# Attention block on one core: a quarter of x transposed by TensorE and the rest by transfers, output weights loaded late, order of work picked among 24

## The chip, the core and the metric

The kernel runs on one core of a Trainium2 chip. The metric is device time in microseconds (us), as the median of repeated executions. One further execution was taken with the hardware profiler; views of the profile are from it. Engines are named as in the profile: PE is TensorE (matmuls), PEld its weight loads, DVE is VectorE, ACT is ScalarE, POOL is GpSimd, SP is SyncE, which here only issues transfers (DMAs). "L298" is line 298 of the kernel.

## The reference

Multi-head self-attention in bfloat16, with S = 2048 positions, D = 448 channels, 16 heads of 28 channels:

```python
B, S, D, H = 1, 2048, 448, 16
Dh = D // H
qkv = (x @ wqkv).reshape(B, S, 3, H, Dh).transpose(2, 0, 3, 1, 4)
q, k, v = qkv[0], qkv[1], qkv[2]
scores = jnp.einsum("bhqd,bhkd->bhqk", q, k) * (Dh ** -0.5)
p = _softmax(scores, axis=-1)
o = jnp.einsum("bhqk,bhkd->bhqd", p, v)
return o.transpose(0, 2, 1, 3).reshape(B, S, D) @ wo
```

## The kernel before

**Tiling.** The 16 heads form four groups g of four (G, HG); each head takes 32 of the 128 partitions (HP), 28 of them for its channels and four for helper rows. The 2048 queries form four chunks c of 512 (QW, NQC), the keys 16 tiles of 128 (NKT). A set is one group with one chunk, and there are 16 sets (NSET). In a set there are 4 heads x 16 key tiles of scores, each 128 keys by 512 queries, which makes 1024 such units in the whole kernel. A unit's exponential is made on one of two engines. ScalarE takes two units at a time (`do_exp`, L928, 128x1024, result `pt`). VectorE takes one unit (`do_a`, L943, result `I`): it makes the exponential out of integer arithmetic on the bits of a bfloat16, and a sum of three shifted copies improves it, for which the copies `J` are made, four units at once, by an addition on VectorE (`do_add`, L1014) or by a clear on GpSimd (L979) and an accumulating transfer issued there (L990). Each result is multiplied with V into the set's output bank `o` (L1073). V carries a column of ones, so that the denominators come out with it.

**Start.** x has to lie with its channels on partitions (`XT`) before anything can be projected. x arrives in four blocks of 512 positions (`load_x`, L140, halves issued by SP and by ACT's queue) with the positions on partitions, in `xs`. Block b takes the positions t + 16p. TensorE transposes each block in 16 pieces against `ident` (`xt_job`, L621, 112 channels x 128 positions each), into two PSUM banks; ScalarE copies one (L629) and VectorE the other (L627) to `XT`. The weights arrive as `WG` (columns of group 0, of K and Q; L143) and as `WRAW` (L136; three loads of 392 KB by SP).

For the softmax no maximum of the scores is taken, but a bound: for each head the largest norm of a key times the norm of the query. So the first scores need all four blocks of K for group 0 (`k_first`): projection (L298, a train of 16 matmuls), square on ScalarE (L324), norm by a matmul with `blockK` (L409), maximum on VectorE (L414), and after the last of the four the maximum over all (L418), a root (L420) and, with the norm of Q (`qn_first`, L487, L491), the bound `su` (L496). Then the first score matmuls (L730) and the first exponential (L928) can run. Until the projected Q and its bound have been placed in the tiles `QP` by small transfers of SP (`rows_first` L661, `place` L502), each score is made of two matmuls, one with `z` and one with `su`; afterwards it is one with `QP` (function `wide`).

Each tile `QP[c][k][z]` (16 of them) has rows with a constant (OFFS). VectorE clears all 16 tiles (L194), and SP issues 16 small transfers that write the constant rows (L198). GpSimd makes `ident`, clears V's tiles (L209, L210), clears the output weights' tile `WO` (L216) and issues 16 transfers that load it (L219).

**Rest.** Projections for groups 1 to 3, V, norms and the output projection of finished chunks (`oproj_job`) lie between the score matmuls in bank `m`. A finished set's output is evacuated (L1100), its denominators are gathered, inverted and spread by SP's transfers through DRAM (L1105, L1114, L1120), and GpSimd multiplies (L1123). The end of the kernel is written by hand (L1293 on): last normalisation, last output projection, last stores.

**What sets the order.** The order on each engine is fixed when the kernel is built. A planner in the kernel (from L234 on) keeps a clock for each engine in `free`, a table `evt` of the times at which inputs are due (L636: x block 0 at 4.9, block 1 at 6.2, 8.0, 9.3 and so on), durations for each job (`add`, the class `Op`) and priorities (`pri`), and issues whatever its pick functions choose next (`pick_pe`, `pick_act`, `pick_dve`, `pick_pool`, `pick_sp`). On the chip every engine works through its list in that order and waits where an input is late.

## Time and profile before

| | |
|---|---|
| median of 3 runs | 361.7 us (361.55 to 361.82) |
| profiled execution, its time | 361.72 us |
| profiled execution, its span | 359.9 us |
| mean granted TensorE clock | 0.998 |
| first exponential on ScalarE starts | 19.39 us |
| last exponential on ScalarE starts | 350.2 us |
| share of the span: PE, DVE, ACT, POOL | 95%, 93%, 95%, 47% |
| first 20 us: PE, DVE, ACT, POOL busy | 18.13, 15.54, 11.03, 18.43 us |

The span is the time from the first to the last instruction that the profiler saw; the time of the execution holds a little more. In the profile's lists an entry names line, engine, operation, output tile <- input tiles with their sizes, and how many of them (x16). "[0.68 <-PE a L730]" behind a timeline entry means that the engine stood idle for 0.68 us before it, and that a matmul of L730 into tile `a` ended that. The chain of waits follows the end of the run back from instruction to what released it.

The transfers of the start, from the timeline of SP (start, duration of the issues, what):

| start | duration | what | issues |
|---|---|---|---|
| 0.74 | 0.86 | x, first halves (L140) | 2 |
| 1.64 | 0.43 | first K weights (L143) | 1 |
| 2.12 | 2.66 | x, further halves | 2 |
| 6.05 | 1.46 | full weights (L136) | 3 |
| 7.63 | 11.51 | constant rows of QP (L198) | 16 |
| 19.24 | 3.22 | rows of Q, from z (L661) | 4 |
| 22.56 | 1.09 | bound, from su (L502) | 2 |

### The profile page before, as it was taken

The numbers are of one execution on the slowest core, as the hardware profiler recorded it, in microseconds if no ns is written. First come the engines' busy times: TensorE is split into PE (matmuls) and PEld (weight loads), VectorE is DVE, ScalarE is ACT, GpSimd is POOL, SyncE is SP. The second block draws the span as 40 slices with busy tenths as digits, with TensorE's granted clock in tenths as the row PEclk, the third lists the DMA queues.
The fourth block names the chain that finished last, engine by engine and source line by source line (L and its number), as shares of the span: only waits on it lengthen the run. The fifth ranks groups of instructions, "written<-read, shape, count | busy, mean of one in ns | idle before, by whom it ended". The sixth has DMA issues, their size and how long they took to land.

```text
span 359.9 us, 11256 instructions
## 1 busy us (share of the span) xinstructions
PE 343.1 (95%) x4520; PEld 111.3 (31%) x4521; DVE 335.4 (93%) x617; ACT 341.1 (95%) x373; POOL 170.2 (47%) x213
## 2 busy tenths in 40 slices
PE   8999999999999999999999999999889999999995
PEld 4533233332234322332232222222222222222233
DVE  8689999999989999999899999999999999999863
ACT  3789999999999999999999999999999999999991
POOL 8951353655444483545635765465546362521010
PEclk9999999999999999999999999999999999999999
DMA  8620063555636765365577646377857685672111
GB/s 242 142 47 15 21 125 86 113 107 105 135 75 129 148 124 113 89 132 108 117 143 149 120 91 137 78 152 158 177 116 156 128 176 129 142 147 66 34 51 54
DMA packets 24017, 41.17 MB, mean 114 GB/s; under 512 B 8604, under 2 KB 15004, under 8 KB 23964
## 3 DMA queue, kind: packets, MB, share of 16 engines
q0 software_dynamic: 8432, 29.24, 42.0%
q1 hardware_dynamic: 14348, 10.07, 10.3%
q10 hardware_dynamic: 1184, 1.14, 1.0%
q8 instruction: 35, 0.57, 0.6%
q14 instruction: 18, 0.15, 0.1%
HBM read 7.58 MB, written 1.96 MB: 27 GB/s over the span
## 4 chain that ended last, share of the span: by engine, by line
PE 37%; ACT 30%; DVE 23%; issue 9%; DMA 1%; DVEq 0%; ACTq 0%
ACT pt L928 30%; PE a L730 12%; DVE I L943 10%; PE o L1073 10%; PE m L305 5%; DVE J L1014 5%; PE m L298 4%; DVE V L579 2%; DVE V L566 2%; DVE KA L338 1%; PE o L643 1%; PE d L730 1%; DVE QA L460 1%; DVE o_sb L1100 1%; PE d L621 1%
## 5 line engine op out<-in xcount | busy, mean ns | idle before, releaser
L928 ACT ACTIVATE pt<-a 128x1024 bf16<-128x1024 f32 x358 | 329.7, 1129 | 2.9 <-PE a L730 1.3
L943 DVE TENSOR_SCALAR I<-d 128x512 int16<-128x512 f32 x278 | 181.0, 680 | 10.1 <-PE d L730 8.8
L730 PE MATMUL a<-QP,KA 32*128 32x512 bf16 (+1 forms) x704 | 137.3, 381 | 8.9 <-ACT pt L928 8.0
L1073 PE MATMUL o<-pt,V 128*32 128x512 bf16 x716 | 105.2, 384 | 0.0
L730 PE MATMUL d<-QP,KA 32*128 32x512 bf16 (+1 forms) x273 | 95.7, 383 | 0.8 <-DVE I L943 0.2
L730 PEld LDWEIGHTS <-KA 32*128 32x128 bf16 (+1 forms) x1041 | 46.1, 91 | 143.5 <-issue 141.7
L990 POOL DMA_DIRECT2D J<-I x55 | 49.6, 902 | 73.0 <-DVE I L943 49.6
L1073 PE MATMUL o<-J,V 128*32 128x512 bf16 x616 | 82.7, 384 | 0.0
L979 POOL MEMSET J<- 128x1024 int32 x55 | 60.1, 1094 | 36.7 <-PE d L730 12.0
L1014 DVE TENSOR_SCALAR J<-I 128x2048 int16<-128x2048 int16 x99 | 73.9, 764 | 0.6
L1073 PE MATMUL o<-I,V 128*32 128x512 bf16 x308 | 64.3, 384 | 0.1
L1073 PEld LDWEIGHTS <-V 128*32 128x32 bf16 x1640 | 30.8, 94 | 48.2 <-issue 45.1
L1123 POOL TENSOR_TENSOR xs<-o_sb,rr 128x512 bf16<-128x512 f32 x12 | 16.9, 1404 | 27.3 <-DVE J L1014 26.9
L298 PE MATMUL m<-XT,WRAW 112*32 112x512 bf16 x384 | 29.6, 384 | 0.2 <-DVE QA L460 0.2
L320 POOL TENSOR_TENSOR sq<-QA 128x512 bf16<-128x512 bf16 x15 | 16.8, 1122 | 23.1 <-DVE QA L460 17.8
L305 PE MATMUL m<-WRAW,XT 112*32 112x112 bf16 (+1 forms) x768 | 20.7, 230 | 0.3 <-DVE KA L338 0.3
L943 DVE TENSOR_SCALAR I<-m 128x512 int16<-128x512 f32 x30 | 20.3, 678 | 0.0
L320 POOL TENSOR_TENSOR sq<-KA 128x512 bf16<-128x512 bf16 x12 | 14.2, 1185 | 9.4 <-DVE J L1014 8.5
L305 PEld LDWEIGHTS <-XT 112*32 112x32 bf16 x768 | 12.3, 96 | 11.5 <-issue 11.4
L305 PE MATMUL m<-WO,xs 128*32 128x448 bf16 x156 | 12.5, 358 | 0.0
L730 PE MATMUL m<-QP,KA 32*128 32x512 bf16 (+1 forms) x30 | 11.5, 384 | 0.0
L460 DVE CAST QA<-m 128x512 bf16<-128x512 f32 x15 | 10.2, 683 | 0.7 <-PE m L298 0.7
(116 smaller groups left out, 207.3 us busy)
## 6 DMA issues: line engine op xcount, KB each, us to landing
J<-I POOLq DMA_DIRECT2D x55, 512.0 KB, 4.9
rr<-scr SPq DMA_DIRECT2D x60, 64.0 KB
QP<-QA SPq DMA_DIRECT2D x60, 28.0 KB
out_dram<-osb SPq DMA_DIRECT2D x12, 112.0 KB
WRAW<-in_wqkv_dram SPq DMA_DIRECT2D x3, 392.0 KB
xs<-in_x_dram ACTq DMA_DIRECT2D x4, 224.0 KB
xs<-in_x_dram SPq DMA_DIRECT2D x4, 224.0 KB
QP<-su SPq DMA_DIRECT2D x32, 2.0 KB
```

The costliest lines, as they stand in the source:

```text
L298: nc.tensor.matmul(out=ps[HP * i:HP * (i + 1), :], lhsT=w[:, cc, h * Dh:h * Dh + HP], rhs=XT[c][cc // 2][:, cc % 2, :], start=(cc == 0), s ...
L305: nc.tensor.matmul(out=out[r, :], lhsT=lhsT[:, r], rhs=rhs, start=start, stop=stop, tile_position=(0, HP * i), **k)
L320: after_shared(nc.gpsimd.tensor_tensor(out=t[:], in0=src, in1=src, op=ALU.mult))
L460: nc.vector.tensor_copy(out=t[:], in_=held[key][:, 0:QW])
L730: nc.tensor.matmul(out=out_ap, lhsT=KAt[(g, j // XB)][r, (j % XB) * P:(j % XB + 1) * P], rhs=q[r, :], start=(n == 0), stop=(n == len(terms ...
L928: nc.scalar.activation(out=pt[:], in_=ps[:], func=ACT.Exp, scale=LN2 / 128.0)
L943: nc.vector.tensor_scalar(out=dst, in0=pd[:], scalar1=BIAS, scalar2=0.0, op0=ALU.add, op1=ALU.max)
L979: m = nc.gpsimd.memset(ch[1][:].bitcast(I32), fill)
L990: after_shared(nc.gpsimd.dma_start(out=ch[1][:, w], in_=ch["I"][:, w], accum_op=ALU.add))
L1014: cur["shared"] = nc.vector.tensor_scalar(out=r[:, w], in0=ch["I"][:, w], scalar1=float(SHIFT[k]), scalar2=None, op0=ALU.add)
L1073: nc.tensor.matmul(out=o[HP * i:HP * (i + 1), :], lhsT=VT[e["k"]][g, j // XB][:, j % XB, HP * i:HP * (i + 1)], rhs=e["ap"], start=(SETMM[k ...
L1123: m = nc.gpsimd.tensor_tensor(out=otile(g, c), in0=st["o_sb"][:], in1=st["rr"][:], op=ALU.mult)
```

## The change

- **x.** Block 0 (NPL = 1) still comes with positions on partitions and is transposed by TensorE, in 16 pieces of 128 channels. Blocks 1 to 3 are transposed by transfers that SP issues (`dma_start_transpose`) straight from DRAM into `XT`: one for each block with channels 0 to 383, and one, ahead of these, for channels 320 to 447 of all three blocks (`XE`). The channels now form chunks of 128 (CK), and the last chunk repeats 64 channels of the one before; the weights that meet them there are zero rows. The blocks are now 512 consecutive positions each, and the output is stored accordingly (`out_at`).
- **Weights.** Each weight load is two transfers (three full chunks, and the last 64 channels). The first columns of K and Q are issued by ACT's queue; V's full weights by SP behind the transposing transfers; Q's and K's full weights by SP as planner jobs after the first placing of Q (`need=["QP00"]`). VectorE and GpSimd clear the zero rows.
- **Constant rows of QP.** VectorE clears only the eight tiles for even groups; GpSimd clears the other eight and issues the transfers of the constant rows, but for the two of chunk 0, which SP issues.
- **Output weights.** GpSimd's clears of `WO` and its 16 loads leave the start. They are planner jobs now: four clears on GpSimd after the bound of the last chunk of group 0, and 16 loads issued by SP.
- **First norms.** The banks of the first norms and the priority of the first Q projection change (QPRI 3.15 to 3.05).
- **Schedule.** The planner is now a function `plan`. It is run 24 times (NSEED) without building anything (`Dry` swallows every call), each time with another seed that shifts two of VectorE's decisions by a random amount, of up to 0.4 in one and up to 1.0 in the other; seed 0 shifts nothing. The one whose clocks end first is then built. Due times in `evt` are changed to fit the new loads.

The diff without changes of indentation, cut to its core:

```diff
-    CK = D // CC
+    CK = P
+    CT = D - CK
+    NPL = 1
+    NSEED = 24
...
+    XT += [big.tile([CK, CC - 1, QW], BF16, name=f"XT{b}") for b in range(NPL, NXB)]
+    XE = big.tile([CK, 1, S - NPL * QW], BF16, name="XE")
...
+    def load_w(t, eng, n=D):
+        dst = WG[t] if n < D else WRAW[t][:, :, 0:D]
+        cols = slice(t * D, t * D + n)
+        eng.dma_start(out=dst[:, 0:CC - 1, :], in_=wqkv[0:(CC - 1) * CK, cols].rearrange("(cc p) n -> p cc n", p=CK))
+        eng.dma_start(out=dst[CC * CK - D:CK, CC - 1, :], in_=wqkv[(CC - 1) * CK:D, cols])
+    def load_x(b):
+        rows = slice(b * QW, (b + 1) * QW)
+        nc.sync.dma_start_transpose(out=XT[b][:], in_=x2[rows, 0:(CC - 1) * CK])
...
+    for t in range(2):
+        nc.vector.memset(WG[t][0:CC * CK - D, CC - 1, :], 0.0)
+    for t in (1, 0):
+        load_w(t, nc.scalar, HG * Dh + WPAD)
+    nc.sync.dma_start_transpose(out=XE[:], in_=x2[NPL * QW:S, CT:D])
+    for b in range(NPL, NXB):
+        load_x(b)
     load_w(2, nc.sync)
-    load_w(0, nc.sync)
-    load_w(1, nc.sync)
...
-            for z in range(2):
-                nc.vector.memset(QP[c][k][z][:], 0.0)
-    for z in range(2):
-        for c in range(NQC):
-            for k in range(2):
-                nc.sync.dma_start(out=QP[c][k][z][HP * k + Dh + NQC - 1 - c:P:2 * HP, :], in_=offs)
+            nc.vector.memset(QP[c][k][0][:], 0.0)
+    def offs_rows(c, z, eng):
+        for k in range(2):
+            eng.dma_start(out=QP[c][k][z][HP * k + Dh + NQC - 1 - c:P:2 * HP, :], in_=offs[:])
+    nc.gpsimd.memset(offs[:], OFFS)
+    offs_rows(0, 0, nc.sync)
...
     for t in range(3):
         nc.gpsimd.memset(WRAW[t][:, :, D:D + WPAD], 0.0)
+        nc.gpsimd.memset(WRAW[t][0:CC * CK - D, CC - 1, 0:D], 0.0)
...
-    for gg in range(G):
-        nc.gpsimd.memset(WO[:, gg, :], 0.0)
-    for h in range(H):
-        g, i = divmod(h, HG)
-        nc.gpsimd.dma_start(out=WO[HP * i:HP * i + Dh, g, :], in_=wo[h * Dh:(h + 1) * Dh, :])
+    for c in range(1, NQC):
+        offs_rows(c, 0, nc.gpsimd)
+    for c in range(NQC):
+        for k in range(2):
+            nc.gpsimd.memset(QP[c][k][1][:], 0.0)
+    for c in range(NQC):
+        offs_rows(c, 1, nc.gpsimd)
...
+    def plan(nc, tc, psum, big, wk, dram, seed, dry):
+        rnd = random.Random(seed)
+        def shake(w):
+            return rnd.uniform(-w, w) if seed else 0.0
...
-    QPRI = 3.15
+        QPRI = 3.05
...
-    for n, t in (("x", 0), 4.9), (("G", 1), 6.9), (("G", 0), 6.9), (("x", 1), 6.2), (("x", 2), 8.0), (("x", 3), 9.3), \
-            (("W", 2), 10.9), (("W", 0), 12.0), (("W", 1), 13.2):
+        for n, t in [(("x", 0), 4.9), (("x", 1), 99.0)] + [(("XT", k, h), 8.9 + 1.8 * (k - NPL)) for k in range(NPL, NXB) for h in range(2)] + \
+                [(("G", 1), 6.7), (("G", 0), 6.7), (("W", 2), 14.2)]:
...
+        def load_wo(h):
+            g, i = divmod(h, HG)
+            nc.sync.dma_start(out=WO[HP * i:HP * i + Dh, g, :], in_=wo[h * Dh:(h + 1) * Dh, :])
+        for gg in range(G):
+            add("POOL", 0.5, lambda gg=gg: clear_wo(gg), need=[("QA", 0, CL)], gives=[("WZ", gg)], pri=95, port=True)
+        for h in range(H):
+            add("SP", 0.55, lambda h=h: load_wo(h), need=[("WZ", h // HG)], gives=[("WO", h)], pri=9, land=2.5)
...
-    k_first(0, "a0", None, "DVE", "ACT", 1.5)
-    k_first(1, "a1", "o", "ACT", "ACT", 3.05, late=("ksq", 0, NQC - 1))
-    k_first(2, "d0", "a0", "ACT", "ACT", 3.1, late=("ksq", 0, NQC - 1))
-    k_first(3, "d1", "o", "DVE", "ACT", 3.2, late=("QA", 0, 0))
+        k_first(0, "a0", "o", "DVE", "ACT", 1.5)
+        k_first(1, "a1", "a0", "ACT", "ACT", 3.05, late=("ksq", 0, NQC - 1))
+        k_first(2, "d0", "o", "ACT", "ACT", 3.1, late=("ksq", 0, NQC - 1))
+        k_first(3, "d1", "a0", "DVE", "ACT", 3.2, late=("QA", 0, 0))
-    qn_first("a0", 3.3)
+        qn_first("o", 3.15)
+        for t in range(2):
+            add("SP", 1.2, lambda t=t: load_w(t, nc.sync), need=["QP00"], gives=[("W", t)], land=6.0, pri=3)
...
-        return fin <= free["ACT"] + D_EXP * (len(exps) + max(0, left() // 2 - 2)) + 0.2
+            return fin <= free["ACT"] + D_EXP * (len(exps) + max(0, left() // 2 - 2)) + 0.2 + shake(0.4)
...
-        if can_add and t > adds[0][0]["at"] + AGE:
+            if can_add and t > adds[0][0]["at"] + AGE + shake(1.0):
...
+    d = Dry()
+    ends = {k: plan(d, d, d, d, d, d, k, True) for k in range(NSEED)}
+    seed = min(ends, key=lambda k: ends[k])
+    plan(nc, tc, psum, big, wk, dram, seed, False)
```

More of the change, by code (lines that the diff above doesn't have):

```diff
@@ new lines, in turn, with do_s @@
+        def turn(t):
+            return max(t, cur["c_end"] + D_TURN)
+        def do_s(t):
+            s = act_set()
+            if s >= NSET:
+                return None
+            q = qa_ready(s)
+            if q is None or q > t:
+                return None
+            got = d_more(s, t, True) if left() >= 16 or chain["cur"] is not None else []
+            used = {g[2][1] for g in got}
+            step = []
+            for x in range(2):
+                own = [i for i in (2 * x, 2 * x + 1) if i not in used and remain[s][i]]
+                step.append(take(s, max(own, key=lambda i: (len(remain[s][i]), (i + cur["u"]) % 2))))
+            bank = s_bank()
+            ps = pair_tile(bank)
+            emit_s([(ps[:, k * QW:(k + 1) * QW], step[k]) for k in range(2)] + [(g[1][:], g[2]) for g in got], t)
+            outst[s] += 2
+            res[bank] = None
+            t = turn(t)
+            end = t + D_S
+            exps.append((end + LATS[("PE", "ACT")], ps, bank, step))
+            cur["u"] += 1
+            cnt["half"] += 2
+            return max(end, put_d(got))
@@ new lines, in plan, with filler @@
+        if dry:
+            return max(free.values())
+        s = NSET - 1
+        g, c = set_gc(s)
+        o = cur["o"]
+        HW = QW // 2
+        banks = held["early"]
+        more = sorted((op for op in ops["PE"] if op.gives[0][0] == "E"), key=lambda op: op.gives[0][1:])
+        def filler(n, to=XB):
+            for op in [op for op in more if op.gives[0][1] < to][:n]:
+                op.emit()
+                more.remove(op)
+        osb_last = [VT[1][0, hf].rearrange("p t e -> p (t e)").bitcast(F32) for hf in range(2)]
```

1924 lines of the change are left out of this document (945 added, 979 removed).

## The prediction

> **What bounds the kernel now.** I read the page first, then the chain of waits, the timeline of the first 25 us, and ScalarE's part of it. The sum below is made against the profiled execution: its time is 361.72 us for a span of 359.9 us, so 1.8 us lie around the span; the median of the runs shown is 361.7 us, the same to 0.02.
>
> The page:
>
> ```profile
> span 359.9 us, 11256 instructions
> PE 343.1 (95%) x4520; PEld 111.3 (31%) x4521; DVE 335.4 (93%) x617; ACT 341.1 (95%) x373; POOL 170.2 (47%) x213
> L928 ACT ACTIVATE pt<-a 128x1024 bf16<-128x1024 f32 x358 | 329.7, 1129 | 2.9 <-PE a L730 1.3
> L943 DVE TENSOR_SCALAR I<-d 128x512 int16<-128x512 f32 x278 | 181.0, 680 | 10.1 <-PE d L730 8.8
> ```
>
> Three engines are full, and ScalarE's 358 exponentials (L928) are one unbroken train. They begin at 19.39 and end at 350.2 + 1.02 = 351.3; 8.6 us of final projection and store follow. In the chain of waits their floor is visible:
>
> ```profile
> 82.16 0.77 ACT pt L928
> ...
> 90.29 0.92 ACT pt L928
> ```
>
> Nine of them in 8.13 us: 0.903 us each. So the span is: start of the train, plus 358 places at 0.903 or a little more, plus a tail. ScalarE filtered from the timeline shows how the train starts:
>
> ```profile
> 19.39 1.94 ACT L928 ACTIVATE pt<-a 128x1024 bf16<-128x1024 f32 x2 [0.68 <-PE a L730]
> 21.51 1.94 ACT L928 ACTIVATE pt<-a 128x1024 bf16<-128x1024 f32 x2 [0.19 <-PE d L730]
> 23.67 1.02 ACT L928 ACTIVATE pt<-a 128x1024 bf16<-128x1024 f32 x1 [0.22 <-PE d L730]
> 24.95 35.85 ACT L928 ACTIVATE pt<-a 128x1024 bf16<-128x1024 f32 x39 [0.25 <-PE d L730]
> ```
>
> Up to 24.95 five places take 5.56 us instead of 5 x 0.903 = 4.52. From there, 353 places take 351.27 - 24.95 = 326.3 us, 0.924 each: 7.3 us above the floor, spread over the run.
>
> What sets 19.39 is the chain of waits from 5.64 on (start, duration, what):
>
> ```profile
> 5.64 1.49 PE d L621 x16
> 7.13 0.45 PE o L621 x8
> 7.57 0.45 PE m L621 x8
> 8.02 0.98 PE a L298 x16
> 9.00 1.03 PE d L621 x16
> 10.03 0.98 PE a L298 x16
> 11.01 0.58 PE o L621 x8
> 11.59 0.21 PE a L409
> 11.81 0.45 PE m L621 x8
> 12.25 0.98 PE d L298 x16
> 13.23 0.32 PE o L409
> 13.55 0.98 PE m L298 x16
> 14.53 0.32 PE a L409
> 14.85 1.01 PE d L298 x16
> 15.94 0.70 ACT sq L324
> ```
>
> TensorE alone is the path from 5.64 to 15.86: transposes (L621), four projections of K and one of Q (L298), norms (L409). After the last K projection come square, norm, maximum, root and bound, and the first exponential starts 4.6 us after that projection started (14.78 to 19.39 in the timeline).
>
> **The change part by part.**
>
> *Transposes of blocks 1 to 3.* 48 of the 64 TensorE transposes go, with three copies of 1.01 us on ScalarE and three of 0.68 on VectorE. Behind the first K projection the chain holds 1.03 + 0.58 + 0.45 = 2.06 us of them; the two groups ahead of it (0.45 + 0.45) go too, but the first projection still waits for the copies of block 0 (ScalarE's ends at 7.54, VectorE's at 7.86), so nothing is won there. In the built program's order the norm of Q now stands ahead of the last K projection (0.32 more) and one filler matmul too (0.21), one norm behind it (0.32 less). 2.06 - 0.21 gives 1.85: the last K projection could start at 14.8 - 1.85 = 12.9, and the train 4.6 later, at 17.5. **-1.8 us**, if the transposing transfers have landed by 12.9.
>
> *When they land* no row shows: the trace has no such transfer. They read 1536 x 448 values and 64 columns twice, 1.57 MB, behind block 0 (0.46 MB) and the first weights (0.21 MB), all on the same 16 engines. Plain loads begin to move at about 1.7 us. From both sides: at the 384 GB/s that the windows of 1 us show between 3 and 4 all 2.24 MB are in by 1.7 + 5.8 = 7.5; at the rate of the 512 KB accumulating transfers of GpSimd (J<-I, 4.9 us to landing, 107 GB/s) the transposes alone take 14.7 us after some 2 us for the rest, so 18.4. I take the row of the weights that arrive in 896-byte pieces (9 to 13 us, 246 to 251 GB/s), since pieces of 768 and 256 bytes are nearest to it: 6.3 us, landing near 10 (1.7 + 2 + 6.3), and up to 12.9 costs nothing. SyncE issues the last two only when block 0 is in (4.99), which leaves that as it is. The Trainium skill states 261 GB/s for such a transfer with a non-contiguous middle dimension (DMA: Bandwidth & Descriptors, Latency and other measured facts); by it the sum would be the same, and no run here shows it.
>
> *First score pairs.* Until the rows of Q are in place (QP), each score is two matmuls, with z and with su. The rows now wait behind 16 small transfers on SyncE (L198, 11.51 us, 0.72 each) and are issued from 19.24. Of the 16, two stay on SyncE and 14 go to GpSimd, so the rows can go when z is there, near 12. Doubled scores fall from 17 to 11 in the program's order. The early loss of 5.56 - 4.52 = 1.04 us shrinks in that ratio, by 0.37. **-0.4 us**; bounds 0 and -1.04.
>
> *GpSimd.* Its prologue ends at 23.0. Out go four clears (1.77) and 16 issues of the output weights (8.54); in come 14 issues at 0.53, eight clears of 128x512 at 0.54, three of 64x448 and the constant at about 0.5: 13.7 for 10.3. It ends near 26.4; its first work after that is a square at 30.08 that waits for VectorE (7.07 idle before it). **0**, hidden by that idle time; without it 3.4 us. VectorE loses eight clears (16 took 4.38, so 2.2) ahead of 7.2, when it only waits for transposes: **0**.
>
> *Weights later.* Six SyncE issues (two for each of three matrices); K's and Q's full weights wait for the first bound (near 17.5), then land within some 4 us; their first use is group 1, beyond 40 us (its squares of K are at 47.4). V's stand behind the last transposing transfer, 0.40 MB at 250 GB/s, 1.6 us, and V's first projection stands some 2 us behind the last K projection. **0**; every microsecond by which V is late there is one of the train's start.
>
> *Output weights.* 16 SyncE issues at 0.4 to 0.83 us (as other rows there) and four GpSimd clears of 0.49, put near 50 us. Queued behind them is the chain of the first denominators (scr, rr): SyncE idles between 49.3 and 55.8 and again to 60.5, so at worst scr goes some 4 us later, and what needs it, the second-next evacuation of an output bank, is 20 us off. **0**; without that cover 4.
>
> *Schedule out of 24.* 358 exponentials on ScalarE, 308 units on VectorE and 99 of its adds are the same counts in both programs. Only order and waits move, so what can be won is part of the 7.3 us above the floor; bounds -3.6 (half of it) and +2.0 (VectorE's waits for scores, 8.8 us in all, up by a quarter). I take a small part, **-0.5**, as a choice and not a reading.
>
> Projections over 128 rows instead of 112 stream the same 512 columns: 0.
>
> Sum: 361.7 - 1.8 - 0.4 - 0.5 = **359.0 us**.
>
> **The rivals.**
>
> *The transfers come late* (slower). Past 12.9 every microsecond of landing is one of start, since the last K projection stands in TensorE's order with all that follows; the change loses from 12.9 + 2.7 = 15.6 on, 1.57 MB in some 12 us or 130 GB/s. [...] At 107: 18.4 instead of 12.9, 359.0 + 5.5 = 364.5. Chance 0.13.
>
> *Block by block.* If each 128x128 block is a step of the queue, as small transfers are (0.72 us each on L198), 48 blocks take 35 us, landing near 37: 359.0 + 24 = 383. Chance 0.02; nothing here shows it. The Trainium skill speaks that way against the change: 1309 ns for a block by transfer beside 390 on TensorE, which it prefers where PSUM can take the result (VectorE: DVE Perf Modes, The three transpose paths). By it 63 us, and a time near 411; of TensorE's side the trace differs, 16 in 1.49 us.
>
> *The new order costs* (not faster). TensorE and VectorE are at 95% and 93%; an order made for other arrival times may stretch the train. If 0.924 became 0.932, 353 x 0.008 = 2.8 us are gone, and the time is 359.5 + 2.8 = 362.3 at the far end, 361.7 in the middle. Chance 0.11.
>
> *The choice brings nothing*, only the start does: 359.5. Chance 0.09.
>
> **How the numbers follow.** The forecast has 0.65, with 357.5 to 360.6 as its own range. Under 0.2% (0.7 us) counts as no change, about what a measurement can tell here. Faster: 0.65 + 0.09 and 0.02 of the third rival, 0.76. Slower: 0.13 + 0.02 and 0.04 of the third, 0.19. Same: 0.05. The range: down to 356.6 (train at 17.0, all 1.04, and 1.9 from the order: -5.2), up to 362.4, which takes in the third rival and the first up to a landing near 16; about 0.13 lie above and 0.06 below.
>
> **What would show it.** Right: the last K projection at 12.5 to 13.2, the first exponential at 17.1 to 17.9 and none of TensorE's waits on XT before it over 0.5 us; 353 places at 0.920 to 0.925; the tail still 8.6. Wrong: TensorE idle before the projection of XT1, XT2 or XT3, or clocked low there; a train that starts early but ends where it did; rows of Q still late, or V's first projection waiting for its weights.

## The result, and the profile after

The changed kernel takes 365.25 us (median of 20 runs, 361.19 to 370.02), the kernel before in the same session 361.73 us (20 runs, 361.19 to 362.26). The ratio is 1.0066, with a 95% interval of 1.0041 to 1.0092: slower, where 359.0 was forecast, and the median lies above the range of 356.6 to 362.4. The four runs above 367 us count as slow and are not in this ratio, so it is smaller than that of the two medians, 1.0097.

The median hides that the 20 runs lie in two heaps. Five take 361.2 to 361.9 us, at a mean granted TensorE clock of 0.999 or 1.0. Fifteen take 364.5 to 370.0 us, at a clock of 0.986 to 0.995. The kernel before has no second heap. The profiled execution belongs to the first: 361.69 us for a span of 359.9, clock 1.0. So its profile can be set against the forecast step by step, but the cause of the 3.5 us has to come from elsewhere.

The page of the changed kernel:

```profile
span 359.9 us, 11136 instructions
PE 337.2 (94%) x4454; PEld 108.1 (30%) x4454; DVE 332.9 (92%) x607; ACT 339.2 (94%) x370; POOL 178.2 (50%) x223
L980 ACT ACTIVATE pt<-a 128x1024 bf16<-128x1024 f32 x358 | 330.6, 1125 | 4.5 <-PE d L782 2.3
L995 DVE TENSOR_SCALAR I<-d 128x512 int16<-128x512 f32 x276 | 180.5, 681 | 10.0 <-PE d L782 8.0
```

TensorE has 66 matmuls and 5.9 us less to do, and the span is what it was. The timeline of ScalarE shows that the start did get shorter:

```profile
16.63 1.94 ACT L980 ACTIVATE pt<-a 128x1024 bf16<-128x1024 f32 x2 [0.70 <-PE a L782]
18.76 6.01 ACT L980 ACTIVATE pt<-a 128x1024 bf16<-128x1024 f32 x6 [0.19 <-PE d L782]
25.09 15.06 ACT L980 ACTIVATE pt<-a 128x1024 bf16<-128x1024 f32 x16 [0.32 <-PE d L782]
```

The first exponential starts at 16.63 instead of 19.39, 2.76 us earlier. (Some 0.7 us of that is luck of this execution; the part on the prediction shows it.) SyncE's timeline and TensorE's, over the last K projection, show why:

```profile
1.20 1.69 SPq L182 DMA_TRANSPOSE XE<-in_x_dram  x1
2.93 6.13 SPq L171 DMA_TRANSPOSE XT<-in_x_dram  x3
11.75 3.87 SPq L711 DMA_DIRECT2D QP<-z  x4
```

```profile
12.03 0.83 PE L337 MATMUL d<-XT,o_sb 128*32 128x512 bf16 x12
```

The four transposing transfers are issued in 7.8 us, and the fourth K projection starts at 12.03. The rows of Q are issued from 11.75 instead of 19.24.

Then the gain is given back. The last exponential starts at 349.78, 0.45 us earlier than before (350.23). Counted against 357 places at the floor of 0.9036 us (most starts in the traces are 0.904 apart), which is 322.59 us, the train before loses 350.23 - 19.39 - 322.59 = 8.25 us, the one after 349.78 - 16.63 - 322.59 = 10.56. From the start of the last exponential to the end of the span it is 10.1 us instead of 9.7. So in the undisturbed execution: start -2.76, train +2.3, end +0.4, together nothing.

Two losses have to be explained: the fifteen runs with the lower clock, and the 2.3 us of the train.

### The profile page after: what moved, and what is told of

Read it like the earlier page. It is cut to its first block, busy times and chain, and to the rows that moved or that the text cites. A ratio compares the mean times of both kernels' runs of the same rounds, so it can differ in the third digit from the quotient of the medians.

```text
span 359.9 us, 11136 instructions
## 1 busy us (share of the span) xinstructions
PE 337.2 (94%) x4454; PEld 108.1 (30%) x4454; DVE 332.9 (92%) x607; ACT 339.2 (94%) x370; POOL 178.2 (50%) x223
## 4 chain that ended last, share of the span: by engine, by line
PE 32%; ACT 27%; DVE 8%; issue 6%; DMA 2%; DVEq 0%; ACTq 0%; POOLq 0%
ACT pt L980 27%; PE a L782 12%; PE o L1125 10%; PE m L344 4%; DVE I L995 4%; PE m L337 3%; DVE J L1066 2%; DMA J<-I 2%; PE d L782 1%; PE d L344 0%; DVE KA L377 0%; DVE kst L397 0%; DVE o_sb L1152 0%; DVE kbc L401 0%; PE o L344 0%
## 5 line engine op out<-in xcount | busy, mean ns | idle before, releaser
L1125 PE MATMUL o<-pt,V 128*32 128x512 bf16 x716 | 108.2, 383 | 0.0
L782 PE MATMUL d<-QP,KA 32*128 32x512 bf16 (+1 forms) x273 | 98.2, 383 | 0.2
L1125 PE MATMUL o<-J,V 128*32 128x512 bf16 x616 | 87.1, 384 | 0.9 <-DMA J<-I 0.5
L1031 POOL MEMSET J<- 128x1024 int32 x55 | 58.4, 1061 | 48.7 <-PE d L782 13.6
L1042 POOL DMA_DIRECT2D J<-I x55 | 52.7, 957 | 57.6 <-DVE I L995 49.6
L1125 PE MATMUL o<-I,V 128*32 128x512 bf16 x308 | 68.2, 383 | 1.0 <-DVE o_sb L1152 0.9
L1175 POOL TENSOR_TENSOR xs<-o_sb,rr 128x512 bf16<-128x512 f32 x12 | 17.1, 1426 | 30.5 <-DVE J L1066 20.1
L337 PE MATMUL m<-XT,WRAW 128*32 128x512 bf16 x216 | 18.3, 386 | 0.1
L344 PE MATMUL m<-WRAW,XT 128*32 128x112 bf16 (+1 forms) x432 | 13.7, 231 | 0.2
L344 PE MATMUL m<-sq,maskK 128*32 128x512 bf16 x108 | 10.8, 389 | 1.9 <-POOL sq L359 1.6
L344 PE MATMUL m<-WO,xs 128*32 128x448 bf16 x156 | 12.5, 359 | 0.0
L1152 DVE COPY o_sb<-o 128x512 f32<-128x512 f32 x15 | 10.2, 681 | 0.8 <-PE o L1125 0.8
```

What stands on the lines that cost most here:

```text
L337: nc.tensor.matmul(out=ps[HP * i:HP * (i + 1), :], lhsT=w[:, cc, h * Dh:h * Dh + HP], rhs=xt(c, cc), start=(cc == 0), stop=(cc == CC - 1), ...
L344: nc.tensor.matmul(out=out[r, :], lhsT=lhsT[:, r], rhs=rhs, start=start, stop=stop, tile_position=(0, HP * i), **k)
L782: nc.tensor.matmul(out=out_ap, lhsT=KAt[(g, j // XB)][r, (j % XB) * P:(j % XB + 1) * P], rhs=q[r, :], start=(n == 0), stop=(n == len(terms ...
L1031: m = nc.gpsimd.memset(ch[1][:].bitcast(I32), fill)
L1042: after_shared(nc.gpsimd.dma_start(out=ch[1][:, w], in_=ch["I"][:, w], accum_op=ALU.add))
L1125: nc.tensor.matmul(out=o[HP * i:HP * (i + 1), :], lhsT=VT[e["k"]][g, j // XB][:, j % XB, HP * i:HP * (i + 1)], rhs=e["ap"], start=(SETMM[k ...
```

## The experiments

Each ratio below is to the kernel before on the same chip. Four theories stood at first. A: the order chosen among 24 is a bad one on the chip. B: with 48 transposes gone TensorE has too little to do in the start, so its clock is taken down. C: the late loads of the output weights, 16 more issues on SyncE in the run, cost 2 to 3 us. D: the transposing transfers land late in some executions. E came out of the traces of the second group: GpSimd's eight clears of QP shut out VectorE.

### The changed kernel again, and the order

again: the changed kernel, unaltered.

> The changed kernel unaltered, to get a profile of an execution with a low granted clock. The 20 first executions fell in two heaps: 361.2 to 361.9 us at a granted clock of 0.999 to 1.0 (5 of 20), and 364.5 to 370.0 at 0.986 to 0.995 (15 of 20). Theory A (the clock drops in the train, where the newly chosen order leaves TensorE too little work): stretches at half clock lie somewhere after 25 us, each some 3 to 4 us long and each costing 1.5 to 4 us. Theory B (the clock drops in the start, where 48 transposes of TensorE are gone): the stretch at half clock lies before 25 us, and the first exponential comes later than 16.6 us, by some 3 us. Both expect a median of 365 +- 1 us.

364.14 us (8 runs, 361.23 to 366.02), ratio 1.0067 [1.0034, 1.0099]. The two heaps are there again, with a run between them at 363.85; a clock of 0.990 to 0.995 goes with the four slowest.

seed0: the order of seed 0, which shifts nothing.

```diff
-    ends = {k: plan(d, d, d, d, d, d, k, True) for k in range(NSEED)}
-    seed = min(ends, key=lambda k: ends[k])
+    seed = 0
```

> The change with the planner's own order (seed 0) in place of the choice among 24. Theory A (the chosen order is at fault): the start of the train stays at 16.6 us, the clock stays at 0.998 or more in nearly all executions, and the median is 359 to 360.5 us. Theory B (the start is at fault, whatever the order): the clock is low in most executions and the median stays at 364 to 366 us. Theory C (moved work, such as the output weights on SyncE and GpSimd's clears, delays squares and accumulating transfers): clock fine, but the train gives back over 2 us again, so 361 to 362 us.

365.06 us (6 runs), 1.008 [1.005, 1.011]; five of the six at a clock of 0.992 to 0.995, the sixth at 361.24 and 1.0. Another order has the same two heaps: theory A falls as the cause of them.

before24: the kernel before, with only the planner's choice among 24 orders added (`plan`, `Dry`, `shake`).

> The kernel before, with nothing but the choice of the order among 24 seeds. Theory A (a chosen order is at fault): slower than before, 363 to 366 us, with a granted clock under 0.996 in many executions. Theory B and C (start or moved work at fault): clock as before, 360.5 to 362 us.

362.12 us (11 runs), 1.0012 [1.0004, 1.0021], clock 0.998 to 1.0 throughout. The choice alone lowers no clock, and in this kernel it costs 0.4 us rather than winning the 0.5 of the forecast.

### Transfers, TensorE's work, the early loads

nowait: the first K projections of blocks 1 to 3 read block 0 instead, and V's weights are issued ahead of the transposing transfers. The keys of these blocks in group 0 are therefore those of block 0.

```diff
+    load_w(2, nc.sync)
     nc.sync.dma_start_transpose(out=XE[:], in_=x2[NPL * QW:S, CT:D])
...
-                                     rhs=xt(c, cc), start=(cc == 0), stop=(cc == CC - 1),
+                                     rhs=xt(0 if first else c, cc), start=(cc == 0), stop=(cc == CC - 1),
```

> The changed kernel, but the first three projections of K for blocks 1 to 3 read block 0 (so the keys of those blocks are wrong in group 0), and V's weights are loaded ahead of the transposing transfers: nothing of the start waits for these transfers any more, TensorE's work is the same. Theory D (in most executions the transposing transfers come later than in the profiled one, TensorE stands idle, its clock falls): clock 0.998 or more throughout and 360.5 to 361.5 us without the upper heap. Theory B (TensorE has too little work in the start, so that its clock falls): as the changed kernel, median 364 to 366, clock 0.99 to 0.995.

365.4 us (12 runs), 1.0076 [1.0046, 1.0106], nine of them at a clock of 0.988 to 0.995. With nothing on the way to the first exponential waiting for the transfers the second heap stays. Theory D falls.

fill: three filler matmuls ahead of each of these three projections.

```diff
+                for _ in range(3 if sc else 0):
+                    nc.tensor.matmul(out=held[key][:, 0:QW], lhsT=zero[:, 0:P], rhs=zero[:], start=True, stop=True)
```

> The changed kernel with three filler matmuls of 512 columns (0.21 us each) on TensorE ahead of each of the first K projections of blocks 1 to 3, 1.9 us in all, in place of the work of the 48 transposes. Theory B (too little work of TensorE in the start): the clock is 0.998 or more and the time 361 to 362.5 us in all executions. Theory D (late transfers): the upper heap stays, median over 363.5.

369.36 us (5 runs), 1.0194 [1.0172, 1.0217], clock 0.981 to 0.99: more work for TensorE makes it worse. That alone does not end theory B, since the fillers move other work too; dveclr, below, does. But this kernel's profile shows the cause at work for the first time, since its profiled execution is a disturbed one. Its timeline, one line each of GpSimd, VectorE, TensorE and ScalarE:

```profile
17.43 3.84 POOL L250 MEMSET QP<- 128x512 bf16 x8
18.27 3.29 DVE L537 TENSOR_SCALAR su<-V,kroot 128x512 bf16<-128x512 f32 x1
...
21.61 0.58 PE L784 MATMUL a<-su,KA 32*128 32x512 bf16 x1 [2.94 <-DVE su L537]
...
22.68 1.94 ACT L982 ACTIVATE pt<-a 128x1024 bf16<-128x1024 f32 x2 [4.01 <-PE a L784]
```

The bound `su` takes 3.29 us on VectorE. In the kernel before it takes 0.49, and so do two scalings of V behind it, beside a GpSimd that issues transfers:

```profile
13.87 8.54 POOL L219 DMA_DIRECT2D WO<-in_wo_dram  x16
...
18.20 0.49 DVE L496 TENSOR_SCALAR su<-V,kroot 128x512 bf16<-128x512 f32 x1
...
19.33 0.49 DVE L579 TENSOR_SCALAR V<-V 128x512 bf16<-128x512 bf16 x2
```

In fill, `su` lies inside GpSimd's row of eight clears and ends 0.29 us after that row (17.43 + 3.84 = 21.27). The first score matmul waits 2.94 us for it, ScalarE 4.01. The fillers had pushed `su` back from 15.45 to 18.27, into the clears.

woearly: the output weights' clears and loads back at the end of GpSimd's start; the planner's jobs for them go.

```diff
+    for gg in range(G):
+        nc.gpsimd.memset(WO[:, gg, :], 0.0)
+    for h in range(H):
+        g, i = divmod(h, HG)
+        nc.gpsimd.dma_start(out=WO[HP * i:HP * i + Dh, g, :], in_=wo[h * Dh:(h + 1) * Dh, :])
```

> The changed kernel with the clears and loads of the output weights back on GpSimd at the start, the order chosen among 24 as in the change. Theory C (the loads in the middle of the run hold up SyncE, and so squares, accumulations and the clock): clock 0.998 or more and 359.5 to 361 us. Theories B and D: median 364 to 366, clock 0.99 to 0.995, as the changed kernel.

366.0 us (5 runs), 1.0116 [1.01, 1.0131], clock 0.986 to 0.993. No gain, and its timeline shows the same hold on another instruction:

```profile
16.75 4.74 DVE L624 TENSOR_SCALAR V<-V 128x512 bf16<-128x512 bf16 x2
16.81 1.94 ACT L984 ACTIVATE pt<-a 128x1024 bf16<-128x1024 f32 x2 [0.76 <-PE a L786]
17.53 3.80 POOL L250 MEMSET QP<- 128x512 bf16 x8
...
24.51 1.02 ACT L984 ACTIVATE pt<-a 128x1024 bf16<-128x1024 f32 x1 [3.63 <-PE d L786]
```

Here the two scalings of V, some 0.5 us together in the kernel before, last 4.74 us, until 21.49; the row of clears ends at 21.33. Both held instructions read and write SBUF alone. This kernel loses once more, later: with the loads added, GpSimd's start lasts until 37.6, and TensorE waits for its next square, so the run decides nothing on theory C:

```profile
38.62 0.40 PE L350 MATMUL m<-sq,maskK 128*32 128x512 bf16 x4 [3.23 <-POOL sq L365]
```

In the changed kernel's own timeline the same instruction slips through:

```profile
16.57 1.01 DVE L618 TENSOR_SCALAR V<-V 128x512 bf16<-128x512 bf16 x2
...
17.68 3.80 POOL L250 MEMSET QP<- 128x512 bf16 x8
...
18.80 0.69 DVE L995 TENSOR_SCALAR I<-d 128x512 int16<-128x512 f32 x1 [0.62 <-PE d L782]
...
20.54 1.29 DVE L618 TENSOR_SCALAR V<-V 128x512 bf16<-128x512 bf16 x2
```

It ends at 17.58, 0.1 us before the clears begin. `I<-d`, which reads PSUM, takes its usual 0.69 us in the middle of the row; the second pair, at 20.54, stands for some 0.8 us until the row has ended. So theory E: a race of a tenth of a microsecond, between this pair and the row, decides which heap an execution falls into. That is inferred: the two profiled executions of the changed kernel are both of the lower heap, and the hold at its full length was seen in its variants only.

### Taking the clears away, and doubling them

dveclr: the eight clears back on VectorE, TensorE's order unchanged.

```diff
+            nc.vector.memset(QP[c][k][1][:], 0.0)
...
-            nc.gpsimd.memset(QP[c][k][1][:], 0.0)
```

> The changed kernel with one part undone: the eight clears of QP for odd groups are back on VectorE in the start; the order is the same to the instruction on TensorE. Theory E (GpSimd's eight clears, a stretch of 3.8 us from 17.5 on, shut out VectorE's fast SBUF-to-SBUF instructions, which stand until the stretch is over; TensorE runs dry and its clock falls in the window after): no heap above 362.5 us any more, granted clock 0.998 or more in all executions, median 360.8 to 361.7 (what the lucky executions of the change show, less or more 0.4 for VectorE's longer start). Theory C (output weights in the middle of the run): the upper heap stays, median over 364.

361.1 us (11 runs, 360.72 to 361.85), 0.9991 [0.9982, 1.0], clock 0.996 to 1.0: the second heap is gone. Its timeline, with GpSimd only issuing transfers beside:

```profile
14.73 7.09 POOL L228 DMA_DIRECT2D QP<-offs  x13
...
17.27 0.49 DVE L618 TENSOR_SCALAR V<-V 128x512 bf16<-128x512 bf16 x2
17.33 1.94 ACT L980 ACTIVATE pt<-a 128x1024 bf16<-128x1024 f32 x2 [0.79 <-PE a L782]
...
21.23 0.52 DVE L618 TENSOR_SCALAR V<-V 128x512 bf16<-128x512 bf16 x2
```

Two scalings take 0.49 us: GpSimd's issues hold up nothing here, its clears, in the same place, did. Theory B falls too: TensorE has the same little work in the start, and its clock stays up.

clr2: GpSimd's eight clears done twice, nothing else.

```diff
     for c in range(NQC):
         for k in range(2):
             nc.gpsimd.memset(QP[c][k][1][:], 0.0)
+    for c in range(NQC):
+        for k in range(2):
+            nc.gpsimd.memset(QP[c][k][1][:], 0.0)
```

> The changed kernel with GpSimd's eight clears made twice (16, 7.6 us). Theory E: what was shut out for up to 3.8 us is now shut out for up to 7.6, so the upper heap moves up by 3 to 5 us, to 368 to 371, and a VectorE instruction of some 4 us or more stands in the trace between 16 and 25 us if its execution is of that heap. Theory C, or any in which these clears only use idle time of GpSimd: 365 +- 1 as the change.

369.85 us (5 runs), 1.0228 [1.0203, 1.0254], clock 0.984 to 0.991, no run in the lower heap. The first pair of scalings got through again, and the second stood through what was left of both rows:

```profile
17.70 3.80 POOL L250 MEMSET QP<- 128x512 bf16 x8
...
20.46 5.13 DVE L621 TENSOR_SCALAR V<-V 128x512 bf16<-128x512 bf16 x2
21.43 3.81 POOL L253 MEMSET QP<- 128x512 bf16 x8
...
28.33 1.02 ACT L983 ACTIVATE pt<-a 128x1024 bf16<-128x1024 f32 x1 [4.73 <-PE d L785]
```

It ends at 25.59, 0.35 us after the second row. With dveclr, theory E is shown: without the clears no second heap, with twice as many nothing but it.

spaced: the same eight clears on GpSimd, but behind every two of them the two issues that belong to them.

```diff
     for c in range(NQC):
         for k in range(2):
             nc.gpsimd.memset(QP[c][k][1][:], 0.0)
-    for c in range(NQC):
         offs_rows(c, 1, nc.gpsimd)
```

> The changed kernel with GpSimd's eight clears of QP no longer in one row: behind every two of them stand the two issues of the constant rows that write into these two tiles, so that the longest row of clears is about 1 us instead of 3.8, and the same instructions stand in the same order on all other engines. Theory E, row form (a fast VectorE instruction stands until the whole row of clears has ended): it now waits at most about 1 us, the granted clock stays at 0.997 or above in most runs, and the median falls to 361.0 to 362.5. Theory E, other form (VectorE is held by each clear alike, however they are spread, or GpSimd's issues hold it too): the hold stays at 3 us or more, the clock at 0.986 to 0.995 and the median at 364 to 366.

362.12 us (12 runs, 360.77 to 365.69), 1.0018 [0.9996, 1.0041]; eleven of the twelve at 0.997 or above. That is the row form: the hold has the length of the row. Four of these eleven still take 363.7 to 364.6 us, at a clock of 0.999 or 1.0, so some time goes without a lower clock; no profile shows where. The profiled execution is the one at 0.995, and its timeline shows three of the four pairs of clears holding one instruction for about a microsecond:

```profile
17.41 1.30 POOL L250 MEMSET QP<- 128x512 bf16 x2
...
17.75 1.31 DVE L617 TENSOR_SCALAR V<-V 128x512 bf16<-128x512 bf16 x2
...
21.72 1.58 DVE L617 TENSOR_SCALAR V<-V 128x512 bf16<-128x512 bf16 x2
21.94 1.01 POOL L250 MEMSET QP<- 128x512 bf16 x2
...
23.93 1.57 DVE L1065 TENSOR_SCALAR J<-I 128x2048 int16<-128x2048 int16 x1
23.94 1.01 POOL L250 MEMSET QP<- 128x512 bf16 x2
```

How such a hold becomes a lower clock is seen in the same kernel's windows (busy time and count of PE, PEld, DVE, ACT, POOL; then the granted clock):

```profile
19.96:23.38 3.42, 3.36 (x88) 1.35 (x81) 3.40 (x6) 3.40 (x4) 3.19 (x7) 1.00 0.79 222
23.38:26.79 3.41, 2.21 (x38) 0.54 (x34) 3.38 (x5) 2.50 (x3) 3.28 (x9) 1.00 0.05 9
26.79:30.20 3.41, 3.41 (x32) 0.52 (x24) 2.63 (x6) 1.92 (x2) 0.00 (x0) 0.50 0.00 0
30.20:33.60 3.40, 3.40 (x85) 1.30 (x82) 3.31 (x6) 3.06 (x5) 1.04 (x1) 1.00 0.07 17
```

In the second window VectorE is late and TensorE is busy for only 2.21 of 3.41 us. In the next the clock is 0.50; TensorE is busy all the time and does 32 matmuls, where the windows around it hold 38 to 88. In clr2 and fill half clock holds for two such windows (25.6 to 32.4 and 20.1 to 27.0). So the hold is paid twice, once as idle time and once as half clock.

### A version that keeps the gain

wosoon: six clears of QP on VectorE in the start, the other two and the clears of `WO` on VectorE behind its copy of block 0; the output weights loaded by SyncE behind the first rows of Q.

```diff
+                    for k in range(2):
+                        nc.vector.memset(QP[NQC - 1][k][1][:], 0.0)
+                    for gg in range(G):
+                        nc.vector.memset(WO[:, gg, :], 0.0)
```

> Clears of QP for odd groups and of the output weights' tile on VectorE (in its idle time of the start), the 16 loads of the output weights issued by SyncE right behind the full weights of Q and K, before 30 us; the order chosen anew among 24. Theory E with C (loads in the middle of the run cost the train 2 to 3 us, as the gap of 2.3 us between an early start and an unchanged end in the lucky executions says): 358 to 359.5 us, clock 0.998 or more. Theory E alone (where the loads stand does not matter, the train is what these orders give): 360.5 to 361.7.

374.96 us (4 runs), 1.0368 [1.0353, 1.0382], and it says nothing of what it was meant for. The two clears came to stand, in the program, behind the transfers that write the constant rows of the same tiles: VectorE waits for these transfers, and the rows are cleared after they were written. Its timeline:

```profile
22.30 0.27 DVE L670 MEMSET QP<- 128x256 uint32 x1 [15.39 <-DMA QP<-offs]
```

best: the same, with these two clears on GpSimd at 4 us, ahead of V's.

```diff
+    for k in range(2):
+        nc.gpsimd.memset(QP[NQC - 1][k][1][:], 0.0)
...
-            nc.gpsimd.memset(QP[c][k][1][:], 0.0)
...
+                    for gg in range(G):
+                        nc.vector.memset(WO[:, gg, :], 0.0)
...
-            add("SP", 0.55, lambda h=h: load_wo(h), need=[("WZ", h // HG)], gives=[("WO", h)], pri=9, land=2.5)
+            add("SP", 0.55, lambda h=h: load_wo(h), need=["QP00"], gives=[("WO", h)], pri=9, land=2.5)
```

> The change without GpSimd's late clears and with early output weights: of the eight clears of QP for odd groups six on VectorE in its idle start and two on GpSimd ahead of V's clears; the output weights' tile cleared by VectorE between its copy of block 0 and the first K (idle there), its 16 loads issued by SyncE behind the full weights of Q and K; order chosen anew among 24. Theory E with C (late clears cost the upper heap, loads in the middle of the run cost the train 2 to 3 us): first exponential near 16.7, 358 to 359.5 us, clock 0.998 or more. Theory E alone: 360 to 361 us.

359.0 us (5 runs, 358.77 to 359.84), 0.9938 [0.9926, 0.995]: faster than both kernels. Its page and ScalarE's timeline:

```profile
span 357.8 us, 11113 instructions
```

```profile
16.89 1.94 ACT L979 ACTIVATE pt<-a 128x1024 bf16<-128x1024 f32 x2 [0.79 <-PE a L781]
19.01 11.34 ACT L979 ACTIVATE pt<-a 128x1024 bf16<-128x1024 f32 x12 [0.19 <-PE d L781]
```

Twelve exponentials run without a break from 19.01, where the changed kernel's train broke after six. The train loses 346.89 - 16.89 - 322.59 = 7.4 us against its floor; from the start of the last exponential to the end it is 10.9 us.

best0: as best, with the order of seed 0 (the edit of seed0).

> The same with the planner's own order (seed 0). If the choice among 24 is worth its own forecast of a gain, this one is 0.5 to 2 us slower than the chosen one; if the chosen order is no better on the chip (as in the kernel before, 0.12% slower by it), it is within 0.7 us or faster.

359.66 us (5 runs), 0.9954 [0.9941, 0.9967]. The choice among 24 seems to be worth 0.66 us here, but the two intervals overlap.

midwo: as best, with the output weights loaded in the run again, near 47 us.

```diff
-            add("SP", 0.55, lambda h=h: load_wo(h), need=["QP00"], gives=[("WO", h)], pri=9, land=2.5)
+            add("SP", 0.55, lambda h=h: load_wo(h), need=[("QA", 0, CL)], gives=[("WO", h)], pri=9, land=2.5)
```

> The same as the first of these, but for the 16 loads of the output weights, which wait for the bound of group 0's last chunk as in the change and so stand near 47 us; order chosen anew among 24. Theory C (those loads hold up the first denominators and with them GpSimd's multiplication and squares): 2 to 3 us slower than the first of these, 360.5 to 362. If not C: within 0.7 us of it.

359.26 us (7 runs), 0.9949 [0.993, 0.9968]. Late loads cost at most some tenths: theory C falls.

### Where the train loses its 2 us

dveclr starts its train at 17.33, 2.06 us earlier than before, and is only 0.6 us faster. Three kernels ask what midwo has that dveclr has not.

dve0: dveclr with the order of seed 0.

> The kernel with all eight clears back on VectorE, and the order of seed 0 instead of the chosen one. What is asked is why that kernel, whose first exponential starts 2.06 us earlier than before, ends only 0.6 us earlier. Theory F (the order chosen among 24 stretches the train in the run, since it was chosen on clocks with other arrival times): with seed 0 the train gives back less, drift at the last exponential 7.3 to 8.5 us instead of 9.28, and the time falls to 359.7 to 360.5. Theory G (GpSimd's four clears of the output weights' tile in the run, or any order over these arrivals, stretch it): drift 9 us or more, and 361.0 to 361.8.

360.89 us (12 runs), 0.9973 [0.9962, 0.9984]; its train, in the profiled execution, the fastest of the twelve, loses 7.9 us (over 359 places; this order has 360 exponentials). Between the two expectations: the chosen order accounts for 0.2 us of the time by the medians and 0.65 by the ratios, whose intervals overlap.

midpool: the changed kernel with only the places of QP's clears as in best (six on VectorE, two on GpSimd at the start), so with GpSimd's four clears of `WO` in the run and the order made around them.

> The changed kernel with its planner's part untouched, so with its chosen order, with the four clears of the output weights' tile by GpSimd near 47 us and the late loads; only six clears of QP are on VectorE in the start and two on GpSimd ahead of V's. Beside the kernel that loads the output weights in the run and clears their tile on VectorE in the start (359.26), it tells what GpSimd's four clears in the run cost, with the order that they bring. Theory G (the clears in the run and the order made around them cost the 1.8 us): 360.7 to 361.3. If they cost nothing: 359.0 to 359.6.

360.66 us (10 runs), 0.9968 [0.9955, 0.9981]: 1.4 us over midwo by the medians, 0.7 by the ratios; midwo differs only in who clears `WO` and when, and in the order that follows. That speaks for theory G, in one of its two forms.

ghost: midpool's order on every engine, but where it has GpSimd's four clears nothing is issued; VectorE clears `WO` in the start. midpool2 is midpool beside it.

```diff
+                    for gg in range(G):
+                        nc.vector.memset(WO[:, gg, :], 0.0)
...
         def clear_wo(gg):
-            nc.gpsimd.memset(WO[:, gg, :], 0.0)
+            pass
```

> As midpool (360.66), with the same order of work on every engine as the planner made it, but where that order has GpSimd's four clears of the output weights' tile nothing is issued; VectorE clears that tile in the start, behind its copy of block 0, as in the kernel that took 359.26. If the four clears themselves cost the 1.4 us between those two: 359.0 to 359.6. If the order that the planner made around them costs it: 360.3 to 361.0.

> midpool once more, beside ghost on the same chip: 360.3 to 361.0 by either theory.

ghost: 359.99 us (5 runs, 359.97 to 360.58), 0.9959 [0.9947, 0.9971]. midpool2: 360.47 us (9 runs, 359.49 to 361.23), 0.997 [0.9959, 0.9982]. ghost lies between its two expectations, and the intervals of midwo, ghost and midpool2 overlap. The three kernels with GpSimd's clears of `WO` in the run (dveclr, dve0, midpool) take 360.5 to 361.1, the three without them or their order (best, best0, midwo) 359.0 to 359.7; how much of that is the clears and how much the order is not settled.

## Why the prediction was wrong

*The step that failed* is the one on GpSimd: "**0**, hidden by that idle time; without it 3.4 us". It asked when GpSimd ends and who waits for its results, and there it was right: its row of clears and issues ended near 26, and nothing waited for it. What it did not ask is whom the instructions hold up while they run. The eight clears fell on 17.7 to 21.5, where VectorE scales V (and in fill, whose start is later, makes `su`); `su` took 3.29 us there (fill), a pair of scalings 4.74 (woearly) or, beside twice the clears, 5.13 (clr2). In the kernel before GpSimd issues transfers from 13.87 to 22.4, and the same instructions take 0.49 beside that. The price, taken from the kernel with the clears back on VectorE, is a ratio of 1.0066 against 0.9991, or 0.75% of 361.7: some 2.7 us; by the medians it is 3.8 (3.5 over the kernel before in one session, 0.3 under it in the other). The step's second half, VectorE's eight clears at 0, holds: dve0, which has them on VectorE again, starts its first exponential at 16.51, the changed kernel at 16.63.

The Trainium skill has the rule that would have raised the question (SBUF — State Buffer, SBUF: two separate sides): a VectorE instruction in a fast mode and a GpSimd instruction share one pair of ports, and whichever starts first keeps the other out until it ends. The traces agree that it is the SBUF-to-SBUF instructions which stand, and `I<-d` out of PSUM which does not. They differ in the length: VectorE got in not after one clear, 0.475 us, but after the whole row.

*The hold is not the whole miss.* Without it, in dveclr, the time is 361.1, still 2.1 above the forecast. There the start and the first score pairs came as forecast (below), but the 349 places behind the first eight take 0.9285 us each, where they take 0.9242 in the kernel before: 1.5 us more, and the end 0.4 more. So the two terms for what comes later, 0 for the output weights and -0.5 for the order, failed together; which of them it is stays open.

*Start of the train*: the step was right, and its surplus is luck. The last K projection started at 12.03, not 12.5 to 13.2, and the first exponential at 16.63, before the 17.1 to 17.9 named: -2.76, where -1.8 was forecast. But TensorE's first work ran at another speed than in the kernel before. The sixteen transposes of block 0 take 1.06 us in the changed kernel:

```profile
5.43 1.06 PE L663 MATMUL d<-ident,xs 128*128 128x128 bf16 x16
```

In the kernel before they take 1.69, and in dveclr, whose line for the last K projection stands below it, 1.70:

```profile
5.43 1.69 PE L621 MATMUL d<-ident,xs 128*112 128x128 bf16 x16
```

```profile
5.56 1.70 PE L663 MATMUL d<-ident,xs 128*128 128x128 bf16 x16
...
12.72 0.83 PE L337 MATMUL d<-XT,o_sb 128*32 128x512 bf16 x12
```

The clock recorded with the traces steps up to full at 5.30 us in the changed kernel's, at 6.76 in that of the kernel before and at 6.89 in dveclr's. So dveclr is the fair comparison with the kernel before: its last K projection starts at 12.72 and its first exponential at 17.33, both within the bounds named, and the gain is 2.06 us. The first exponential of other profiled executions with the new start follows the same step: midpool2 has the step at 4.77 and the exponential at 16.37, best 5.82 and 16.89, midwo 6.81 and 17.28. GpSimd's row of clears begins at 17.4 to 17.7 in all of the profiles that have it, so this step may be what decides the race: in the profiles of the lower heap (the changed kernel, again, seed0, nowait) it comes at 5.13 to 5.30, in woearly, which was held, at 5.56. No run tests that.

*When the transfers land*: right as far as it bears on the sum. Their last packet ends at 11.3 us, not near 10 (1.57 MB in packets of 256 bytes, at 201 GB/s where some 250 was assumed), and before 12.9. TensorE's waits from 5 to 17 us, in the changed kernel, hold one entry, and it is not on XT:

```profile
PE o L448 <- DVE V L530: 0.2, 1, 0.2
```

The columns are total, count and longest. Both rivals built on the transfers fall with it, the second also by the 7.8 us of issues for 48 blocks.

*First score pairs*: the rows were issued at 11.75, as said. In the changed kernel the hold at 20.54 hides what they won: it breaks the train at 24.8 even in the undisturbed execution (8 places take 25.09 - 16.63 = 8.46 us, 1.2 above the floor). In dveclr and best, without a hold, the first eight places lose 0.6, in the kernel before 1.05: 0.45 won, for -0.4 forecast.

*Weights later and late loads of the output weights*: 0 was right for the loads to within some tenths (midwo beside best). GpSimd's four clears that go with them, or the order around them, cost 1.2 to 1.4 us by the medians and 0.7 to 0.8 by the ratios (midpool and midpool2 beside midwo), where 0 stood; the intervals overlap or touch.

*Schedule out of 24*: -0.5 was a choice, and the runs give +0.4 (before24), -0.7 (best beside best0) and +0.2 to +0.65 (dveclr beside dve0). It is small, and of no fixed sign.

*The forecast's 353 places at 0.920 to 0.925*: from 25.09 the changed kernel's 349 places take 349.78 - 25.09 = 324.69 us, 0.930 each. best has 0.923. The rival that the new order costs had the right symptom, a train that starts early and ends where it did, but not the cause of the median: both orders tried show the second heap, and removing eight clears removes it. For the 2.1 us that dveclr still lacks it is not ruled out.

The low end of the range does not add up: its parts are 2.4 + 1.04 + 1.9 = 5.3, not 5.2, and lead to 356.4. Nothing hangs on it.

That 359.0 was reached in the end, by best, is no support for the sum: there the start gives -2.5, the train -0.8 and the end +1.2, and the forecast had no term for the last two but a guess.

## What to carry to other kernels

When work is moved to an idle engine, ask not only who waits for its result but which engine cannot run beside it: here a row of eight GpSimd clears, of tiles that no score needed before group 1, stood in front of 0.5 us of VectorE's work on the critical path. Put such rows where VectorE only reads PSUM or waits, or cut them up with issues of transfers, which held up far less. And when runs fall into two heaps, look for a race of tenths of a microsecond near the critical path; here a profile of the good heap shows the two instructions lying close to each other. Before a difference between two profiles is credited to an edit, see whether the clock stepped up at the same moment in both.

## What was not expected of the hardware

- A row of back-to-back GpSimd clears (8 of 128x512 bf16, 3.80 us) let a waiting SBUF-to-SBUF instruction of VectorE in only at its end: 3.29, 4.74 and 5.13 us for work of 0.5. Pairs of clears held it for about 1 us. GpSimd's issues of transfers held nothing in the kernel before, dveclr and best (0.49 us for two scalings of V beside them), but in the changed kernel, again and clr2 the same pair took 1.0 to 1.1 us while GpSimd still issued transfers and no clear had begun; why is not shown.
- The granted clock fell to 0.50 for the 3.41 us after a window in which TensorE was still busy for 2.21 of 3.41 us (spaced); elsewhere it fell after 1.92 (fill), 1.02 and 1.07 (woearly) and 0.27 us (clr2). The Trainium skill gives the window as 3413 ns and an idle window as the condition for half clock (TensorE: Matmul & The Clock Gate, What's actually happening); the length agrees, and the condition was met here by a window that was far from idle. Busy time alone does not draw the line: the changed kernel has a window of 2.19 us, wosoon one of 2.06, and full clock followed both. The changed kernel's, and the window behind it:

```profile
244.23:247.64 3.41, 2.19 (x28) 0.85 (x26) 3.18 (x7) 2.94 (x4) 0.00 (x0) 1.00 0.69 150
247.64:251.06 3.42, 3.06 (x40) 0.83 (x39) 2.85 (x5) 3.42 (x5) 2.96 (x3) 1.00 0.07 22
```

- 48 blocks of 128x128 were transposed by four transfers within 12 us of the start, beside plain loads, without TensorE waiting for them.
